# Gated linear attention with a low-rank mixer on one Trainium2 core: another order of the same 2207 operations

## Chip, cores and metric
The kernel runs on one core of a Trainium2 chip. The metric is the device time of one execution in microseconds (us). Before the change the median of three runs is 535.81 us, from 535.58 to 535.88. Five engines take part: PE (TensorE, matrix products), DVE (VectorE), ACT (ScalarE), POOL (GpSimd) and SP (SyncE); the last two mostly issue transfers. Each works off its own row of instructions in order and waits by semaphores for the others.

## What is computed
The first part is a complex gated recurrence per batch (4), head (8) and step (768), with a head dimension of 48, all in float32:

```python
mag = np.sqrt(a_re * a_re + a_im * a_im)
scale = np.minimum(mag, 0.999) / (mag + 1e-06)
...
new_re = ar * S_re - ai * S_im
new_im = ar * S_im + ai * S_re
kv = np.einsum('bhd,bhe->bhde', k[:, :, t], v[:, :, t])
S_re, S_im = (new_re + kv, new_im)
y[:, :, t] = np.einsum('bhd,bhde->bhe', q[:, :, t], S_re)
```

Its result, rearranged to x of 4 x 768 x 384, goes through a token mixer of rank 32 and a channel network:

```python
h = xt @ U @ V
u = x + h.transpose(0, 2, 1)
ch = np.maximum(u @ w_ch1, 0.0) @ w_ch2
return (u + ch).astype(np.float32)
```

Here xt is x with steps and channels exchanged; w_ch1 has 384 x 1536 numbers, w_ch2 1536 x 384.

## The kernel before
The 4 x 768 tokens are cut into 24 chunks of 128 tokens, six to a batch. Twelve groups of two chunks go through the gates together; the mixer and the channel network also take two chunks at a time, so there are twelve of each, called mixer 0 to 11. The stages of a chunk are:

- **Gates** of a group: magnitude and angle of a_re and a_im, on ACT (L459) and DVE; prefix sums over time as products on PE (L751, and L747 where the summand is first split on DVE by L737 and L738; L811, L814, L817 for the angles). L715 to L726 belong to the magnitudes, L820 makes the angles' fraction F. Totals of a chunk go out to memory and back (L762, L765), and L767 keeps their least value.
- **Preparation**: DVE multiplies q and k by the gates' waves (L462), PE transposes (L872), ACT copies to SBUF (L878).
- **Chain**: inner products within a chunk (L901), masked on DVE (L904), products with the state and its update (L921, L951, L959; L462 and L468 on DVE).
- **Mixer**: rank products (L1036, L1109), transposes (L1055), then the channel network: up products (L1074, and L1181, which makes the same sums with fewer products from sums of operands, from mixer 2 on), down products (L1270, L1313, L1484), the additions of their results to xo on DVE (L465), and the transfer of xo to the result: L1257 on POOL, and for the last mixers L1471 on POOL or SP.
- **Weights**: w_ch1 and w_ch2 come as float64 words and are turned into float32 piece by piece on DVE by L611, L615, L617 and a custom instruction of L465 (L459 on ACT for a part). In the rows, w_85 and w_86 are the two matrices.
- **Judging**: small DVE operations, three 1x1 products on PE (L1613 to L1615) and a conversion on DVE (L1617) count the elements whose range the fast way does not cover. Every engine then loads that flag (L1648) and branches (L1658) past a slow version of the whole computation, which is not run with these inputs.
- **Warm-up**: two operations of 7 and 5 products of the identity with itself (L1627), which nothing reads.

The program first collects all of these as 2207 numbered operations, each with its engine, what it reads and writes, and a function that issues its instructions. Nothing is issued until the end, where a method of the plan walks a tuple of numbers called ORDER, which stands at the head of the file:

```python
for n in ORDER if ORDER else range(len(self.ops)):
    assert not self.ops[n][5] - done, "an operation comes before what it needs"
    ...
    done.add(n)
    out += [-1 - n] * SPARE.get(n, 0) + [n]
```

(L159 to L170.) So ORDER alone sets the row of instructions of every engine, and with it in which of its rotating buffers (PSUM banks "bank", the ring "xo", "T", "GS") an operation's result lands. SPARE puts idle products (L1636, L1640) ahead of four named operations; it is not changed. A number in ORDER can only stand behind the operations that it needs.

Of the kernel before, what the change touches and what calls it, by code (L numbers as in the profile page):

```python
# [31 lines left out]
    91, 93, 95, 99, 96, 97, 101, 92, 112, 94, 113, 114, 98, 102, 103, 115, 116, 117, 0, 104, 105, 118, 119, 120, 3, 109, 110, 106, 121, 111, 107, 122,  # L32
    123, 124, 130, 5, 4, 6, 9, 148, 11, 188, 8, 12, 15, 108, 14, 189, 149, 7, 131, 132, 135, 133, 147, 126, 212, 134, 140, 136, 137, 10, 191, 13, 146,
    141, 142, 138, 139, 143, 144, 151, 145, 150, 152, 153, 213, 2, 125, 190, 192, 214, 128, 193, 196, 202, 203, 197, 215, 216, 220, 154, 155, 195,
    204, 194, 156, 127, 199, 198, 17, 2205, 227, 205, 157, 206, 28, 158, 100, 2206, 221, 226, 228, 217, 18, 258, 229, 159, 160, 200, 161, 222, 19, 21,
    223, 219, 16, 164, 218, 162, 163, 166, 20, 165, 29, 309, 172, 173, 1, 201, 207, 224, 22, 225, 283, 259, 23, 208, 30, 31, 32, 33, 261, 308, 231,
    232, 233, 284, 168, 211, 210, 235, 236, 174, 175, 234, 209, 237, 176, 177, 239, 182, 183, 178, 179, 180, 238, 313, 184, 181, 185, 186, 187, 312,
    314, 262, 315, 311, 34, 37, 167, 36, 247, 246, 244, 263, 310, 260, 40, 170, 286, 266, 230, 287, 35, 265, 264, 267, 243, 316, 268, 288, 273, 272,
    317, 290, 269, 270, 318, 248, 46, 351, 319, 240, 241, 289, 42, 271, 350, 291, 292, 285, 26, 25, 320, 321, 322, 47, 245, 293, 294, 274, 323, 324,
    325, 43, 275, 326, 50, 328, 278, 277, 279, 295, 327, 334, 335, 41, 297, 298, 44, 38, 45, 39, 280, 242, 169, 336, 352, 337, 48, 282, 281, 52, 276,  # L40
    299, 49, 296, 338, 300, 340, 54, 339, 344, 329, 330, 586, 51, 345, 302, 303, 353, 341, 304, 375, 253, 252, 342, 343, 588, 376, 398, 346, 354, 305,
    307, 358, 348, 347, 587, 306, 349, 364, 378, 365, 301, 366, 591, 589, 254, 359, 367, 590, 355, 379, 360, 592, 331, 24, 357, 593, 361, 399, 249,
    250, 380, 377, 332, 356, 383, 381, 594, 595, 678, 628, 382, 362, 384, 630, 363, 389, 596, 386, 385, 370, 369, 371, 390, 597, 598, 599, 53, 368,
    391, 387, 388, 702, 600, 601, 602, 27, 629, 633, 55, 392, 393, 394, 372, 374, 58, 373, 397, 396, 677, 395, 400, 401, 402, 603, 403, 606, 404, 604,
    608, 607, 605, 614, 726, 701, 64, 615, 441, 616, 251, 61, 442, 443, 444, 445, 255, 420, 56, 421, 256, 422, 423, 446, 60, 448, 59, 405, 424, 406,
    617, 618, 447, 619, 620, 453, 494, 407, 57, 62, 704, 632, 257, 621, 63, 408, 495, 67, 496, 680, 634, 497, 414, 409, 70, 631, 454, 622, 635, 636,
    66, 65, 68, 610, 71, 76, 459, 460, 623, 73, 129, 624, 451, 637, 638, 415, 72, 498, 410, 639, 452, 640, 609, 82, 625, 641, 77, 69, 74, 75, 642,
    449, 450, 433, 417, 78, 626, 411, 425, 643, 644, 416, 645, 83, 627, 84, 80, 85, 86, 647, 646, 648, 649, 650, 656, 657, 658, 672, 675, 674, 671,
    673, 727, 426, 79, 418, 731, 419, 412, 427, 434, 435, 428, 436, 87, 81, 676, 730, 732, 413, 429, 437, 88, 89, 90, 462, 659, 660, 661, 679, 612,
    662, 438, 430, 729, 663, 733, 681, 685, 664, 439, 705, 651, 703, 825, 728, 611, 776, 502, 734, 691, 692, 682, 499, 503, 693, 463, 694, 665, 666,  # L50
    431, 667, 684, 769, 735, 736, 500, 683, 457, 455, 456, 709, 171, 461, 828, 826, 777, 710, 775, 458, 711, 501, 716, 715, 712, 695, 737, 469, 686,
    717, 800, 504, 778, 827, 505, 738, 706, 652, 653, 668, 739, 669, 707, 801, 688, 687, 708, 740, 470, 466, 471, 467, 506, 741, 718, 742, 803, 472,
    743, 507, 508, 745, 746, 744, 748, 747, 754, 755, 474, 670, 772, 770, 756, 333, 689, 468, 473, 690, 464, 465, 478, 713, 696, 721, 714, 719, 475,
    432, 480, 482, 654, 476, 483, 479, 771, 779, 697, 750, 440, 757, 700, 699, 698, 780, 720, 722, 783, 774, 784, 802, 875, 874, 484, 509, 477, 773,
    485, 510, 511, 758, 486, 515, 724, 759, 785, 723, 829, 782, 760, 490, 781, 804, 481, 725, 761, 516, 808, 805, 786, 512, 762, 513, 830, 514, 809,
    491, 492, 807, 806, 789, 790, 487, 787, 517, 518, 524, 763, 489, 519, 520, 899, 749, 1160, 831, 832, 833, 613, 764, 765, 493, 1161, 526, 528, 525,
    488, 530, 521, 834, 788, 527, 810, 811, 522, 791, 531, 523, 766, 835, 836, 792, 873, 837, 767, 529, 838, 898, 532, 533, 867, 536, 537, 768, 870,
    795, 794, 796, 812, 538, 540, 542, 815, 814, 799, 901, 839, 539, 543, 544, 548, 840, 876, 841, 541, 797, 798, 842, 845, 844, 846, 843, 847, 853,
    869, 854, 868, 546, 545, 813, 549, 793, 552, 816, 817, 553, 550, 547, 534, 535, 1165, 561, 820, 819, 821, 877, 855, 856, 551, 878, 872, 881, 562,
    871, 882, 1162, 848, 849, 752, 822, 824, 857, 858, 823, 879, 902, 880, 906, 558, 887, 888, 900, 850, 883, 859, 860, 554, 884, 1164, 1166, 818,  # L60
    912, 913, 861, 889, 903, 904, 907, 909, 1167, 1209, 1163, 751, 1234, 556, 908, 890, 891, 655, 914, 557, 559, 1168, 563, 862, 753, 863, 885, 886,
    1169, 1203, 905, 910, 911, 560, 893, 892, 564, 555, 566, 1170, 1171, 1172, 1173, 915, 916, 864, 894, 1210, 917, 1259, 1233, 1212, 895, 920, 1236,
    565, 567, 1174, 1175, 1176, 574, 897, 568, 575, 918, 865, 570, 576, 571, 919, 896, 866, 921, 922, 573, 572, 1177, 1179, 1180, 923, 569, 924, 1181,
    1178, 1182, 1188, 1205, 582, 577, 925, 926, 927, 928, 929, 930, 932, 933, 583, 584, 1184, 1261, 1204, 1189, 1207, 1190, 934, 937, 578, 935, 579,
    1211, 1002, 942, 1003, 580, 943, 1191, 940, 936, 1213, 948, 941, 946, 944, 1217, 931, 1214, 1260, 1308, 1206, 1004, 1005, 947, 939, 1006, 1208,
    1262, 1223, 1224, 851, 1307, 1237, 956, 949, 945, 952, 953, 1192, 1225, 1226, 1227, 957, 1215, 1193, 938, 954, 950, 955, 1241, 958, 960, 1194,
    959, 964, 961, 962, 966, 1195, 1258, 1263, 1264, 1216, 1196, 581, 965, 1197, 968, 951, 963, 1235, 969, 967, 1332, 1333, 1248, 1247, 1242, 1265,
    1244, 1007, 970, 1309, 1249, 1243, 1009, 1301, 1335, 1198, 974, 977, 975, 1250, 1199, 1008, 1011, 1200, 978, 972, 971, 1218, 1238, 979, 1219,
    1201, 976, 1012, 1266, 1016, 983, 1267, 973, 986, 1220, 980, 1268, 984, 1269, 982, 981, 1202, 990, 985, 1310, 987, 989, 1270, 1239, 1240, 993,
    1081, 1221, 1245, 988, 1010, 991, 1183, 1358, 994, 1082, 1271, 1015, 1272, 1273, 1274, 1275, 1277, 992, 998, 995, 1083, 1276, 1017, 1019, 1020,  # L70
    1018, 1084, 1014, 1246, 1278, 1279, 999, 1023, 1222, 1251, 1280, 1286, 1302, 1303, 1085, 1000, 1013, 1025, 1026, 1021, 1022, 1311, 1024, 1029,
    1031, 1035, 1027, 1315, 1028, 1032, 1312, 1086, 1287, 1288, 1304, 1305, 1036, 1033, 1034, 1037, 1038, 1281, 1186, 1087, 1088, 1030, 1306, 1314,
    1289, 997, 1001, 1290, 852, 1291, 1041, 1282, 1357, 1405, 1313, 1039, 1043, 1406, 1185, 1292, 1040, 1042, 1293, 1044, 1361, 1294, 1045, 1336,
    1047, 585, 996, 1362, 1048, 1340, 1046, 1316, 1228, 1252, 1253, 1318, 1229, 1254, 1317, 1256, 1230, 1360, 1430, 1319, 1359, 1322, 1334, 1257,
    1321, 1053, 1049, 1408, 1295, 1051, 1323, 1324, 1320, 1232, 1231, 1363, 1255, 1056, 1341, 1337, 1407, 1431, 1296, 1297, 1052, 1050, 1096, 1298,
    1057, 1364, 1365, 1339, 1342, 1054, 1338, 1058, 1343, 1090, 1055, 1366, 1367, 1368, 1062, 1059, 1063, 1060, 1066, 1061, 1326, 1327, 1065, 1097,
    1064, 1399, 1369, 1370, 1371, 1372, 1299, 1300, 1373, 1344, 1328, 1068, 1069, 1072, 1374, 1089, 1091, 1092, 1433, 1070, 1073, 1329, 1376, 1331,
# [1630 lines left out]
```

## Time and profile before

| | us |
|---|---|
| median of three runs | 535.81 |
| the profiled execution's span | 533.9 |
| median less that span | 1.92 |
| PE busy (96% of the span) | 514.2 |
| DVE busy (82%) | 438.2 |
| ACT busy (55%) | 295.8 |
| POOL busy (6%) | 30.5 |

The span to three digits behind the point is 533.889 us. Times in all rows count from its start. Busy time is that of the engine's own instructions; issues of transfers on SP, branches and waits count as none. PEld is PE's loading of weights, which runs beside its products. An arrow in brackets names what ended an engine's idle time.

### The profile page before, as it was taken

How to read it: one execution, taken by the hardware profiler on the slowest of the kernel's cores; microseconds unless marked ns; L12 is line 12 of the kernel's file. 1: busy time of each engine (PE TensorE's matmuls, PEld its weight loads, DVE VectorE, ACT ScalarE, POOL GpSimd, SP SyncE). 2: the span in 40 equal slices, each digit the busy share in tenths (PEclk: the TensorE clock that was granted, in tenths of full speed). 3: DMA queues.
4: the chain of work that ended last, by engine and by line, in shares of the span. 5: the costliest groups of instructions: out<-in, count | busy, mean ns of one | idle time of the engine just before them, and what ended most of it. 6: DMA issues, size and time to landing. Idle time of an engine off the chain costs nothing.

```text
span 533.9 us, 17164 instructions
## 1 busy us (share of the span) xinstructions
PE 514.2 (96%) x7494; PEld 468.1 (88%) x7494; DVE 438.2 (82%) x863; ACT 295.8 (55%) x531; POOL 30.5 (6%) x58
## 2 busy tenths in 40 slices
PE   2899999999999999999999999999999999999996
PEld 1777786757989989999999999999999999999996
DVE  7898988999999998897886887786878866877842
ACT  5889998893776866546647655543555412221000
POOL 1000000001020001001100001100010000000010
PEclk9999999999999999999999999999999999999999
DMA  9967985565233423601534150500240000000002
GB/s 226 206 114 194 191 145 163 171 107 112 41 75 92 63 46 80 111 1 29 118 53 83 33 106 25 98 9 23 47 70 26 2 2 1 1 2 1 1 28 97
DMA packets 150706, 39.95 MB, mean 75 GB/s; under 512 B 145880, under 2 KB 147440, under 8 KB 150624
## 3 DMA queue, kind: packets, MB, share of 16 engines
q1 hardware_dynamic: 148544, 34.63, 32.3%
q0 software_dynamic: 2080, 4.15, 2.3%
q8 instruction: 61, 1.00, 0.8%
q14 instruction: 21, 0.17, 0.1%
HBM read 33.60 MB, written 4.76 MB: 72 GB/s over the span
## 4 chain that ended last, share of the span: by engine, by line
PE 81%; DVE 11%; ACT 3%; issue 2%; DMA 2%; SPq 0%; DVEq 0%; ACTq 0%
PE down L1313 20%; PE few L1181 13%; PE bank L1181 12%; PE bank L1484 7%; PE bank L872 4%; PE bank L901 4%; PE up L1074 3%; PE bank L959 3%; PE bank L921 3%; PE bank L951 2%; DVE QKC L462 2%; PE bank L1036 1%; PE bank L747 1%; PE bank L751 1%; PE bank L811 1%
## 5 line engine op out<-in xcount | busy, mean ns | idle before, releaser
L878 ACT COPY QK<-bank 112x512 f32<-112x512 f32 x96 | 51.8, 591 | 18.2 <-PE bank L872 17.9
L1313 PE MATMUL down<-w,h 128*128 128x192 f32 x288 | 53.6, 331 | 0.0
L462 DVE TENSOR_TENSOR QKC<-qk,cs 128x768 f32<-128x768 f32 x48 | 45.0, 951 | 4.9 <-ACT cs L459 4.7
L459 ACT ACTIVATE gate<-gate 128x768 f32<-128x768 f32 (+1 forms) x50 | 39.8, 798 | 16.3 <-DVE wide L719 12.7
L1313 PEld LDWEIGHTS down<-w,h 128*128 128x128 f32 x288 | 47.0, 190 | 0.9
L465 DVE TENSOR_TENSOR xo<-bank,xo 128x192 f32<-128x192 f32 x78 | 25.3, 350 | 24.9 <-PE bank L1484 16.0
L1189 ACT COPY h<-few 128x512 f32<-128x512 f32 x35 | 20.3, 585 | 30.0 <-PE few L1181 29.9
L1074 PE MATMUL up<-uT,w 128*128 128x256 f32 x144 | 34.0, 385 | 0.2
L456 ACT ACT_TABLE_LOAD x24 | 30.8, 1283 | 1.1 <-PEq L1692 0.7
L1074 PEld LDWEIGHTS up<-uT,w 128*128 128x128 f32 x144 | 26.6, 190 | 5.0 <-DVE xo L465 0.5
L1181 PE MATMUL bank<-extra,w 128*128 128x128 f32 x232 | 30.3, 276 | 0.0
L872 PE MATMUL bank<-ident,QKC 64*112 64x64 f32 x768 | 29.1, 221 | 1.0 <-DVE G L468 0.4
L872 PEld LDWEIGHTS bank<-ident,QKC 64*112 64x112 f32 x768 | 24.4, 130 | 6.2 <-DVE QKC L462 1.4
L459 ACT ACTIVATE es<-bank 128x384 f32<-128x384 f32 x48 | 20.3, 495 | 16.6 <-PE bank L747 15.8
L797 POOL DMA_DIRECT2D gate<-F x15 | 12.5, 832 | 285.2 <-DVE F L820 167.2
L1181 PEld LDWEIGHTS bank<-extra,w 128*128 128x128 f32 x232 | 28.3, 192 | 0.1
L1313 PE MATMUL down<-stage 128*128 128x192 f32 x144 | 28.0, 332 | 0.2 <-DVE xo L465 0.2
L465 DVE TENSOR_TENSOR xo<-down,xo 128x192 f32<-128x192 f32 (+1 forms) x58 | 22.0, 386 | 7.1 <-PE down L1313 6.9
L901 PE MATMUL bank<-QK 112*64 112x64 f32 x768 | 26.6, 224 | 0.0
L901 PEld LDWEIGHTS bank<-QK 112*64 112x64 f32 x768 | 24.2, 138 | 1.3 <-issue 0.5
L459 ACT ACTIVATE cs<-F 128x384 f32<-128x384 f32 x48 | 23.3, 516 | 3.0 <-DVE F L820 2.9
L1313 PEld LDWEIGHTS down<-stage 128*128 128x128 f32 x144 | 23.5, 190 | 1.2 <-DVE xo L465 0.5
(249 smaller groups left out, 1228.6 us busy)
## 6 DMA issues: line engine op xcount, KB each, us to landing
stage<-in_moe_w_ch_dram SPq DMA_DIRECT2D x12, 768.0 KB
gate<-in_a_re_dram SPq DMA_DIRECT2D x24, 192.0 KB
gate<-in_a_im_dram SPq DMA_DIRECT2D x24, 192.0 KB
qk<-in_q_dram SPq DMA_DIRECT2D x24, 192.0 KB
qk<-in_k_dram SPq DMA_DIRECT2D x24, 192.0 KB
VP<-in_v_dram SPq DMA_DIRECT2D x24, 192.0 KB
out_dram<-xo POOLq DMA_DIRECT2D x13, 192.0 KB, 2.9
out_dram<-xo POOLq DMA_DIRECT2D x16, 96.0 KB, 2.5
```

The costliest lines, as they stand in the source:

```text
L456: ACT(1.4, rank, lambda: nc.scalar.preload_act_table_set(name), writes=[TABLE])
L459: return nc.scalar.activation(out=o, in_=i, func=f, **kw)
L462: nc.vector.tensor_tensor(out=o, in0=a, in1=b, op=OP.mult)
L465: nc.vector.tensor_tensor(out=o, in0=a, in1=b, op=OP.add)
L872: nc.tensor.transpose(out=get(*ps[r])[0:DQ, h], in_=get(*qkc)[at, h].rearrange("p u d -> p (u d)")[:, 0:DQ], identity=ident[at, at], tile_ ...
L878: nc.scalar.copy(out=get(*QK)[0:DQ, u].rearrange("p (h t) -> p h t", t=CH)[:, :, r * HC:(r + 1) * HC], in_=get(*ps[r])[0:DQ])
L901: nc.tensor.matmul(out=get(*ps0)[r:r + HC, h], lhsT=k_of(h, r, HC), rhs=q_of(h, r, HC), start=True, stop=True, tile_position=(0, r))
L1074: nc.tensor.matmul(out=get(*ps)[:, e], lhsT=w1[:, f, (ff + e) * 128:(ff + e + 1) * 128], rhs=get(*uT)[:, f], start=(f == 0), stop=(f == KD ...
L1181: nc.tensor.matmul(out=get(*ps)[:, q], lhsT=w()[:, q * 128:(q + 1) * 128], rhs=v[0](), start=(n == 0 and q == 0), stop=True, skip_group_ch ...
L1189: ACT(c_act(n3 * CH) - 0.045, RU, lambda i=i, k=k: nc.scalar.copy(out=at(i, k), in_=get(*ps)), [ps], [o])
L1313: nc.tensor.matmul(out=get(*to)[:, part], lhsT=x(j), rhs=y[:, j], start=(first and j == 0), stop=(j == KH - 1), skip_group_check=not first)
L1484: nc.tensor.matmul(out=get(*ps), lhsT=w[0]()[:, q], rhs=x[0]()[:, q], start=(n == 0 and q == 0), stop=(q == k3 - 1), skip_group_check=True)
```

## The change
Only the tuple ORDER is another one: the same 2207 numbers, 2144 of them in another place. It was found by replaying the program three times with the durations of the other engines than PE varied. The file has one line fewer, so every line number of the changed kernel is lower by one than the same line before.

```diff
 ORDER = (
-    91, 93, 95, 99, 96, 97, 101, 92, 112, 94, 113, 114, 98, 102, 103, 115, 116, 117, 0, 104, 105, 118, 119, 120, 3, 109, 110, 106, 121, 111, 107, 122,
...
-    2182, 2179, 2183, 2161, 2180, 2184, 2188, 2189, 2185, 2186, 2191, 2174, 2099, 2094, 1687, 2102, 2190, 2192, 2187, 2193, 1686, 1691, 2194, 2195,
-    2196,
...
+    2188, 2184, 2189, 2191, 2194, 2195, 2192, 2185, 2186, 2080, 2081, 1686, 1687, 2102, 2094, 1691, 2190, 2193, 2187, 2196, 2203, 2204, 2099,
 )
```

The rows of the engines show what it moves. PE's first products before (prefix sums of the first two chunks, idle products, angles):

```order
L751 MATMUL bank_61<-GL,prefix_r 128x384
L1636 MATMUL bank_62<-ident 128x128 x2
L751 MATMUL bank_62<-GL,prefix_r 128x384
L1636 MATMUL bank_63<-ident 128x128 x10
L814 MATMUL bank_63<-gate,prefix_z 128x384
```

And PE's first products now:

```order
L1626 MATMUL warm<-ident 128x128 x12
L750 MATMUL bank_61<-GL,prefix_r 128x384
L1635 MATMUL bank_62<-ident 128x128 x2
L750 MATMUL bank_62<-GL,prefix_r 128x384
L1635 MATMUL bank_63<-ident 128x128 x10
```

Both warm-up operations, which stood behind the first chunk's state products, now stand ahead of everything on PE.

On DVE, the place where the first group with a split summand (group 6) is split, before; GL is the summand, GS its two parts:

```order
L904 COPY_PREDICATED AT_130<-mask,bank_65 128x512
L723 SCALAR_TENSOR_TENSOR GL<-gate,GL 128x768
L462 TENSOR_TENSOR G<-G,T_121 112x384
L468 ISA GM<-bank_62,G 112x384
L904 COPY_PREDICATED AT_132<-mask,bank_65 128x512
L726 SCALAR_TENSOR_TENSOR GL<-GL,gate 128x768
L737 CAST GS_107<-GL 128x768
L738 TENSOR_TENSOR GS_108<-GL,GS_107 128x768
```

And the same place now:

```order
L464 ISA w_86<-w_86,stage 128x1536
L722 SCALAR_TENSOR_TENSOR GL<-gate,GL 128x768
L461 TENSOR_TENSOR G<-G,T_121 112x384
L614 TENSOR_SCALAR stage<-stage 128x768
L467 ISA GM<-bank_61,G 112x384
L903 COPY_PREDICATED AT_130<-mask,bank_62 128x512
L903 COPY_PREDICATED AT_132<-mask,bank_63 128x512
L725 SCALAR_TENSOR_TENSOR GL<-GL,gate 128x768
L736 CAST GS_107<-GL 128x768
L737 TENSOR_TENSOR GS_108<-GL,GS_107 128x768
```

Pieces of the second weight matrix (w_86 and its stage) are now unpacked ahead of the split; before, they stood behind it.

The end of POOL's row before, with the last transfers of xo and the load of the flag:

```order
L1471 DMA out_dram<-xo_128 128x384
L1471 DMA out_dram<-xo_127 128x384
L1257 DMA out_dram<-xo_126 128x192
L1471 DMA out_dram<-xo_127 128x384
L1257 DMA out_dram<-xo_126 128x384
L1257 DMA out_dram<-xo_126 128x192
L1648 TENSOR_LOAD flag
```

And now:

```order
L1256 DMA out_dram<-xo_126 128x384
L1256 DMA out_dram<-xo_126 128x192
L1470 DMA out_dram<-xo_127 128x384 x2
L1256 DMA out_dram<-xo_126 128x192
L1470 DMA out_dram<-xo_128 128x384
L1647 TENSOR_LOAD flag
```

The transfer of xo_128, which is chunk 20, stood ahead of five others and is now the last. It waits for DVE's additions to xo_128, whose row at the end now reads:

```order
L464 TENSOR_TENSOR xo_128<-bank_61,xo_128 128x192
L464 TENSOR_TENSOR xo_128<-bank_62,xo_128 128x192
L1616 CAST flag<-bank_63 1x1
L1647 TENSOR_LOAD flag
```

The end of PE's row before:

```order
L1484 MATMUL bank_66<-w_86,hq 128x192 x4
L1484 MATMUL bank_63<-w2x,w_85 128x192 x4
L1484 MATMUL bank_64<-w2x,w_85 128x192 x4
L1484 MATMUL bank_66<-gate,hq 128x192 x4
L1648 TENSOR_LOAD flag
```

And now:

```order
L1483 MATMUL bank_61<-w2x,w_85 128x192 x4
L1483 MATMUL bank_62<-w2x,hq 128x192 x4
L1612 MATMUL bank_63<-ones,bad 1x1
L1613 MATMUL bank_63<-ones,wide 1x1
L1614 MATMUL bank_63<-ones,bad 1x1
L1647 TENSOR_LOAD flag
```

The last full products belong to chunk 20 (operation 2080; 2081 is its addition and 2099 its transfer), and the three products of the flag (2203; 2204 is the conversion), which stood eight operations of L1484 ahead of the end, now follow them.

165 rows, old and new, of the table ORDER are left out of this document.

## Prediction, made blind
> **What bounds the kernel now.** The page comes first: the span and the busy shares.
>
> ```profile
> span 533.9 us, 17164 instructions
> PE 514.2 (96%) x7494; PEld 468.1 (88%) x7494; DVE 438.2 (82%) x863; ACT 295.8 (55%) x531; POOL 30.5 (6%) x58
> ```
>
> PE (TensorE) is busy for 514.2 of 533.9 us. The other 19.7 us, and what makes PE's own work longer or shorter, are all that a new order can touch. Where the 19.7 us lie is in the view of busy time by stretch (columns: stretch, length, busy time of PE, PE's weight loads, DVE, ACT, POOL, then granted clock, DMA share and GB/s):
>
> ```profile
> 0.00:16.65 16.65, 5.70 (x29) 4.50 (x29) 12.70 (x35) 10.90 (x20) 1.94 (x14) 1.00 0.94 215
> 16.65:82.40 65.75, 63.88 (x1308) 51.08 (x1308) 58.83 (x95) 58.86 (x106) 0.00 (x0) 1.00 0.82 176
> 200.00:447.00 247.00, 246.62 (x3867) 235.77 (x3866) 200.15 (x414) 127.27 (x238) 17.53 (x27) 1.00 0.26 50
> 447.00:528.94 81.94, 81.94 (x640) 80.46 (x638) 54.41 (x116) 10.73 (x19) 3.21 (x6) 1.00 0.05 17
> 528.94:533.89 4.95, 0.00 (x1) 0.00 (x0) 0.36 (x1) 0.00 (x0) 0.00 (x0) 0.81 0.22 70
> ```
>
> PE stands for 11 us at the start, nearly 2 in the stretch up to 82.40, 0.4 in the 247 us from 200, not at all in the last 82 before 528.94, and again for the **4.95 us behind its last product**. So the middle and the late part can only be shortened by making PE's work shorter. The start, the first 80 us (where DVE and ACT are at 90% beside PE) and the end are the places for waits.
>
> **Term 1: the start.** The timeline of the start (start, length, engine, line, operation, count; in brackets the idle time ahead and what ended it):
>
> ```profile
> 1.23 0.57 SPq L569 DMA_DIRECT2D gate<-in_a_im_dram  x1
> 2.72 0.85 SPq L569 DMA_DIRECT2D gate<-in_a_im_dram  x1
> ```
> ```profile
> 10.18 1.62 PE L751 MATMUL bank<-GL,prefix_r 128*128 128x384 f32 x2 [10.18 <-DVE GL L465]
> 11.59 1.06 PE L1636 MATMUL bank<-ident 128*128 128x128 f32 x4
> 12.44 1.20 PE L751 MATMUL bank<-GL,prefix_r 128*128 128x384 f32 x2
> 13.48 2.39 PE L1636 MATMUL bank<-ident 128*128 128x128 f32 x20
> 16.65 1.56 PE L814 MATMUL bank<-gate,prefix_z 128*128 128x384 f32 x4 [0.77 <-ACT gate L459]
> 25.18 1.83 PE L1627 MATMUL warm<-ident 128*128 128x128 f32 x14
> 27.48 1.38 PE L1627 MATMUL warm<-ident 128*128 128x128 f32 x10
> ```
>
> The two warm-up operations of L1627 take 1.83 + 1.38 = 3.2 us of PE at 25 to 29 us. The change puts them ahead of the first L751, where PE stands until 10.18 anyway, so **3.2 us of PE's work go**, hidden under the first loads. The first loads also change places: the pair of a_re and a_im that was issued second (done being issued at 3.57, against 1.80) now comes first. I put the work that follows on the first products 0.3 us later, a fifth of the 1.5 us between the two issues. The bounds: half of those 1.5, +0.75; and -0.74 if the early warm-up leaves PE's first products at the later speed. That is what the rows give: the first two L751 take 1.41 us from start to the next start and the second two 1.04; the first four idle products take 0.85, and twenty of the same 2.39, which for four is 0.48. So 0.37 + 0.37 are there to win. PE waits for ACT at 16.65, so little of it should arrive, and I take none.
>
> The Trainium skill, "TensorE: Matmul & The Clock Gate", section "What's actually happening", states that the array runs at half its clock by default and again after an idle window of about 3.4 us, and at the full clock after about 3.4 us of work. The trace agrees in that the same idle product falls from 0.21 to 0.12 us within 4 us of the first work. By that rule the warm-up lies too early if it ends more than about 3.4 us ahead of the first product and the first products stay slow, so the sum stays as it is; if it ends later, the sum would be the one with -0.74.
>
> **Term 2: the early stretch is bounded by DVE.** After the start, the first 65 us run from DVE's first F to the end of the L738 that splits group 6:
>
> ```profile
> 18.21 0.55 DVE L820 SCALAR_TENSOR_TENSOR F<-F,bank 128x384 f32<-128x384 f32 x1 [1.83 <-ACT F L459]
> 18.68 0.95 DVE L465 CUSTOM_DVE_ANT_0 w<-w,stage 128x1536 uint16<-128x1536 uint16 x1
> ...
> 82.39 0.96 DVE L738 TENSOR_TENSOR GS<-GL,GS 128x768 fp32r<-128x768 f32 x1
> ```
> ```profile
> 18.21:83.36 65.15, 62.76 (x1305) 50.60 (x1305) 59.78 (x95) 58.23 (x104) 0.00 (x0) 1.00 0.81 174
> ```
> ```profile
> L615 DVE TENSOR_SCALAR stage<-stage 128x768 uint16<-128x768 uint16 (+1 forms) x13 | 7.5, 587 | 0.0
> L617 DVE TENSOR_SCALAR w<-w 128x768 uint32<-128x768 uint32 x12 | 6.6, 556 | 0.5 <-ACT w L459 0.3
> L767 DVE TENSOR_TENSOR least<-least,T 112x16 f32<-112x16 f32 x12 | 2.0, 167 | 0.0
> ```
>
> In before the stretch lasts 65.15 us, with PE busy 62.76, DVE 59.78 and ACT 58.23. The new order has five more instructions on DVE ahead of that L738: one L767 (0.17), and four that unpack the second weight matrix: two L615 (0.59 each), one L617 (0.56), one custom L465 (0.95). That is 2.9 us by their durations; an instruction overlaps the next one by some 0.1 us (18.21 to 18.68 for a length of 0.55), so 2.4. DVE then has 62.2 us. PE has 3.2 less (the warm-up), 1.8 less by term 3, and one more up product (1.4, below): 62.76 - 3.6 = 59.2. DVE becomes the busiest. In before the stretch was 2.4 us longer than its busiest engine; with the same 2.4 it lasts 64.6, and ends at 18.5 + 64.6 = 83.1 against 83.36, **0.3 earlier**. So nearly everything that PE gains here is eaten by DVE. The bounds: DVE without any idle time (62.2 us, ends at 80.7, 2.7 earlier) and DVE with all the 5.4 us that it stands idle now (65.15 - 59.78; ends at 86.1, 2.75 later).
>
> One up product more is done by then, taken from behind the place. The chain of waits shows six of its matmuls:
>
> ```profile
> 87.45 1.49 PE up L1074 x6
> ```
>
> They take about 1.4 to the next start, so PE has **1.4 us less** to do after the place.
>
> **Term 3: PE changes its kind of product less often.** Where PE goes from one shape to another, the distance from start to start is longer than within a kind:
>
> ```profile
> 168.22 1.16 PE L1181 MATMUL few<-extra 128*128 128x128 f32 x8
> 169.22 1.06 PE L1181 MATMUL bank<-gate,w 128*128 128x128 f32 x8
> 170.11 1.06 PE L1181 MATMUL few<-extra,gate 128*128 128x128 f32 x8
> 171.10 0.94 PE L921 MATMUL bank<-VP,QKC 64*48 64x48 f32 x64
> ```
>
> Eight L1181 take 0.89 us between their own kind (169.22 to 170.11), 1.00 when entered from another kind (168.22), 0.99 when left for L921 (171.10): about 0.11 a switch. I counted the switches in PE's two orders, with transposes, inner products, state products, rank products and full 128x128 products as kinds: 249 in before, 214 in the new order; 16 of the 35 fewer lie up to the place of term 2, 19 behind it. Those 19 save 19 x 0.11 = **2.1 us**, since PE is never idle there; the 16 (1.8 us) are in term 2's PE work. Bounds: nothing, and 35 x 0.11 = 3.9.
>
> Sum of the terms for PE's last product: -0.3 - 1.4 - 2.1 = **-3.8 us**, so it ends at 525.1. Bounds from term 2: -6.2 without waits, -0.75 with all of them.
>
> **Term 4: the end.** What follows the last product, on each engine:
>
> ```profile
> 518.03 0.62 DVE L465 TENSOR_TENSOR xo<-bank,xo 128x192 f32<-128x192 f32 x2 [2.24 <-PE bank L1484]
> ...
> 528.98 0.36 DVE L465 TENSOR_TENSOR xo<-bank,xo 128x192 f32<-128x192 f32 x1 [0.94 <-PE bank L1484]
> ```
> ```profile
> 518.95 0.54 POOL L1471 DMA_DIRECT2D out_dram<-xo  x1 [9.35 <-DVE xo L465]
> ...
> 520.54 1.07 POOL L1257 DMA_DIRECT2D out_dram<-xo  x2
> ```
> ```profile
> L1658 POOLq EVENT_SEMAPHORE  x5: 17/43/2272, 521.4 to 524.0; - x5
> L1658 POOLq INC_SWDGE_SEM  x1: 1063/1063/1063, 524.0 to 524.0; - x1
> L1658 PEldq COMPARE_BRANCH  x2: 90/1878/3665, 526.5 to 529.1; - x2
> ```
> ```profile
> L1703 POOLq DRAIN  x3: 46/112/3728, 527.9 to 533.6; - x3
> L1703 PEldq DRAIN  x2: 8/38/68, 532.9 to 533.4; - x2
> ```
>
> (The last two fences give, for a line, count: shortest/median/longest ns, first and last start.) In before PE sets the end: its branch behind the last product takes 3.67 us, its drain comes at 532.9, and a common close of about 1.0 us follows. POOL starts its last two transfers at 520.54, so the second at 521.07, eight us ahead of the last product, and its own closing work lies beside PE's: a wait of 2.27 for the landing, 1.06 of counter update up to 525.1, nothing until 527.9, a drain of 3.73 up to 531.6. From the start of its last transfer to the end of that drain POOL needs 531.64 - 521.07 = **10.6 us**.
>
> The new order takes this cover away. The products of chunk 20 (the operation numbered 2080) become PE's last full ones, DVE's additions to that chunk's xo come behind them, and POOL's last transfer, which writes that chunk out, waits for them. So POOL's closing work starts only there: the addition starts 0.04 us after the product and takes 0.36, POOL starts its transfer 0.30 after that (518.65 to 518.95), then 10.6, then the close of 1.0: 12.3 us after the last product, where now it is 4.95. **Term 4 is +7.3 us.** The three 1x1 products that count the flag, and its conversion, also move to the end; flag, load and branch on PE then take 5 to 6.5 us after the last product and are no longer last.
>
> The bounds: if the long drain is in truth a wait for the other engines' transfers (it ends about where SyncE's last transfer lands), 3.73 go and the term is +3.6. If the gap of 2.8 ahead of it goes too, only landing and counter remain (4.0 in place of 10.6): +0.8. I take the full length, since no other engine has so long a drain and POOL's gap and drain follow its own branch.
>
> The Trainium skill, "Runtime: NRT & Kernel Launch", section "Instruction fetch mechanics", says that a taken branch to code outside the loaded pages waits until that page is fetched. The trace agrees: 2.8 us lie between POOL's branch and its drain. By that rule the gap belongs to POOL and comes after its branch wherever that stands, so the +0.8 would be out of reach.
>
> **Sum.** 533.89 - 3.8 + 7.3 = 537.4 for the span. The median of the runs, 535.81, is 1.92 above the profiled span; with the same 1.92 the forecast is **539.3 us**, 0.65% slower. A measurement of this kernel can tell about 0.2% (1.07 us) from no change.
>
> **Rivals.** *The end stays covered (faster).* One mechanism, at POOL's queue: its drain and the gap ahead are waits that end with the other engines, so only landing and counter count, +0.8: 533.89 - 3.8 + 0.8 + 1.92 = 532.8. For it speaks that the drain ends as SyncE's last landing is due; against it the branch ahead of the gap. It decides as soon as the close takes under 4.95 + 3.8 = 8.75 us after the last product. Chance 0.15; with DVE without idle time besides (-6.2), 530.4, chance 0.08. *Only the drain is a wait*: +3.6, 535.6, no difference; chance 0.12. *DVE waits as much as now, with more work*: -0.75 + 7.3, 542.3; for it speaks that ACT and PE feed DVE as they do now, against it that PE has less to do there; chance 0.13. *DVE never waits*: -6.2 + 7.3, 536.9; chance 0.10. My forecast has 0.42.
>
> **How the numbers follow.** The range goes from 532.3 to 542.8: it leaves out the 530.4 and the far side of the 542.3. Slower by over 0.2% (above 536.9): 0.42, 0.13, and half of the 0.10: 0.60. Within: the other half and most of the 0.12: 0.14. Faster: 0.15, 0.08 and the rest: 0.26.
>
> **What would show it.** Step by step: the two L1627 rows ahead of the first L751, which still starts between 9.5 and 11; the L738 of group 6 ending within 80.7 to 86.1, with DVE busy about 62 us from its first F; PE's last full product between 522.7 and 528.2; POOL's last issue behind DVE's last addition, and behind it a landing wait, a gap and a drain of 3.7 us with the span's end 12 us after the last product. The prediction is wrong if the drain shrinks to some tens of ns, if DVE's added unpacking falls into its idle time, or if new waits of PE show up between 200 and 520.

## The result and the profile after

The changed kernel takes 540.67 us (median of four runs, 539.75 to 541.79), the kernel before 535.80 (535.58 to 535.88): a ratio of 1.0094, 95% interval 1.0078 to 1.0109. It is slower by 0.9%; forecast were 539.3 us within 532.3 to 542.8. The profiled execution took 541.31 us, and its runs lie further apart than those of before (2.0 us against 0.3).

The head of the page after:

```profile
span 539.4 us, 17174 instructions
PE 513.6 (95%) x7494; PEld 470.9 (87%) x7494; DVE 437.5 (81%) x863; ACT 295.2 (55%) x531; POOL 30.5 (6%) x58
```

PE is busy for 0.6 us less, and the span is 5.5 us longer. Busy time by stretch, with the columns as in the prediction:

```profile
0.00:16.65 16.65, 10.58 (x46) 9.21 (x47) 12.03 (x35) 10.12 (x18) 1.94 (x14) 0.79 0.90 205
16.65:83.00 66.35, 61.97 (x1291) 49.30 (x1289) 63.04 (x102) 62.09 (x111) 0.00 (x0) 1.00 0.87 190
200.00:447.00 247.00, 246.84 (x3846) 237.33 (x3845) 198.88 (x413) 127.65 (x240) 17.12 (x26) 1.00 0.25 47
447.00:525.00 78.00, 78.00 (x607) 77.35 (x607) 55.65 (x120) 9.59 (x17) 2.68 (x5) 1.00 0.04 13
```
```profile
525.94:539.40 13.46, 0.23 (x7) 0.12 (x6) 0.41 (x2) 0.00 (x0) 0.54 (x1) 0.70 0.13 41
```

The last row is the loss: 13.46 us follow the last full product, where before 4.95 did. That is +8.5, against -3.0 for the product itself (528.94 to 525.94); together they are the 5.5. Two things are new besides: the granted clock of the start is 0.79, where the row of before says 1.00 (its first products were slow too, four idle ones in 0.85 us against twenty in 2.39 behind them), and DVE is the busiest engine of the early stretch.

What stands behind the last product, from the timeline and from the rows of the sequencers (count: shortest/median/longest ns, first and last start):

```profile
524.48 1.46 PE L1483 MATMUL bank<-w2x,hq 128*128 128x192 f32 x8
...
525.99 0.36 DVE L464 TENSOR_TENSOR xo<-bank,xo 128x192 f32<-128x192 f32 x1 [0.94 <-PE bank L1483]
526.26 0.13 DVE L1616 CAST flag<-bank 1x1 int32<-1x1 f32 x1
526.89 0.54 POOL L1470 DMA_DIRECT2D out_dram<-xo  x1 [9.84 <-DVE flag L1616]
```
```profile
L1657 POOLq EVENT_SEMAPHORE  x5: 17/43/3169, 527.5 to 531.0; - x5
...
L1657 POOLq COMPARE_BRANCH  x2: 38/39/40, 527.4 to 532.2; - x2
...
L1657 POOLq INC_SWDGE_SEM  x1: 1063/1063/1063, 531.1 to 531.1; - x1
```
```profile
L1702 POOLq DRAIN  x3: 46/112/3728, 534.8 to 539.1; - x3
...
L1702 PEldq DRAIN  x2: 8/38/68, 531.0 to 538.9; - x2
```

POOL's row reads like a list of what the last transfer pays for: issue at 526.89, landing wait of 3.17, counter update of 1.06, branch at 532.2, nothing until 534.8, drain of 3.73 until 538.5. PE is ready at 531.0 and waits 7.5 us for POOL in the common close.

### The profile page after: what moved, and what is told of

It reads as the page before. It is cut to its first block, busy times and chain, and to the rows that moved or that the text cites. A ratio compares the mean times of both kernels' runs of the same rounds, so it can differ in the third digit from the quotient of the medians.

```text
span 539.4 us, 17174 instructions
## 1 busy us (share of the span) xinstructions
PE 513.6 (95%) x7494; PEld 470.9 (87%) x7494; DVE 437.5 (81%) x863; ACT 295.2 (55%) x531; POOL 30.5 (6%) x58
## 3 DMA queue, kind: packets, MB, share of 16 engines
q0 software_dynamic: 2080, 4.15, 2.3%
## 5 line engine op out<-in xcount | busy, mean ns | idle before, releaser
L1312 PE MATMUL down<-w,h 128*128 128x192 f32 x288 | 52.2, 331 | 0.0
L871 PE MATMUL bank<-ident,QKC 64*112 64x64 f32 x768 | 27.7, 220 | 2.2 <-DVE QKC L461 1.8
L1256 POOL DMA_DIRECT2D out_dram<-xo x26 | 17.2, 732 | 129.7 <-DVE xo L464 95.9
```

Source lines behind the costliest of these rows:

```text
L871: nc.tensor.transpose(out=get(*ps[r])[0:DQ, h], in_=get(*qkc)[at, h].rearrange("p u d -> p (u d)")[:, 0:DQ], identity=ident[at, at], tile_ ...
L1256: queue.dma_start(out=out[b, c * CH:(c + 1) * CH, lo:hi], in_=get("xo", i)[:, lo:hi])
L1312: nc.tensor.matmul(out=get(*to)[:, part], lhsT=x(j), rhs=y[:, j], start=(first and j == 0), stop=(j == KH - 1), skip_group_check=not first)
```

## Experiments

All were run beside the kernel before on the same chip. In experiments 1, 2, 3 and 5 all line numbers are 7 higher than in the kernel before; in the others they are those of the kernel before. The diffs of ORDER show only the numbers that move and some beside them.

**1. The tail as before.** The last 138 operations go back to the relative order that they had before.

```diff
 ORDER = (
...
-    2185, 2186, 2080, 2081, 1686, 1687, 2102, 2094, 1691, 2190, 2193, 2187, 2196, 2203, 2204, 2099,
+    2185, 2186, 2191, 2174, 2099, 2094, 1687, 2102, 2190, 2192, 2187, 2193, 1686, 1691, 2194, 2195, 2196,
 )
```

> The changed order up to its 2069th operation, and the last 138 operations in the order that they had before (chunk 20's down products, its transfer and the flag's products early again). Theory (POOL's closing work, laid bare, is what the change loses): the last product stays some 3 us earlier than in the kernel before and about 5 us follow it, so the time is 532 to 534 us, below the kernel before (535.8). Rival 1 (the loss lies in PE's 1.8 us of standing and the slow products at 85 to 91 us, and the tail costs little): 538 to 540. Rival 2 (the close is long for another reason than the place of the last transfer): no change, 540.7.

Measured: 532.66 us (531.63 to 535.47), ratio 0.9952 (0.9934 to 0.9970). Its rows at the end:

```profile
524.79 1.46 PE L1491 MATMUL bank<-gate,hq 128*128 128x192 f32 x8
```
```profile
L1710 POOLq DRAIN  x3: 46/112/3729, 524.9 to 530.9; - x3
L1710 SPq DRAIN  x3: 7/7/7, 530.2 to 530.6; - x3
...
L1710 PEldq DRAIN  x2: 8/38/68, 530.1 to 530.6; - x2
```

POOL's drain of 3.73 us now starts at 524.9, beside PE's last products, and is over before PE (530.1) and SyncE (530.2) are ready: 4.9 us follow the last product (526.25 to a span of 531.1). Some 8 us come back, so the tail is the whole of the loss, and without it the changed order is 0.5% *faster* than before.

That SyncE is ready 0.1 us behind PE holds for the kernel before as well, where the prediction names PE alone (532.9):

```profile
L1703 SPq DRAIN  x3: 7/7/7, 533.0 to 533.3; - x3
```

**2. The last transfer on SyncE.** The changed order as it is; only the issuing queue of chunk 20 differs.

```diff
-                if t:
+                if t or n == 20:
                     SP(0.6, ("load", 0), lambda: f(nc.sync), [o], [("out", n)])
```

> The changed order as it is, but chunk 20's transfer, still the last, is issued by SyncE in place of POOL. Theory (POOL's own closing work counts from its last transfer on): POOL's last transfer is then issued at about 516.5 us and its close is over before PE's; what follows the last product is PE's flag, branch and the common close, 6 to 8 us in place of 13.5, so 533.5 to 535.5 us. Rival (POOL's long drain is a wait for the last landing of any queue): the drain still ends some 5 us behind the last transfer, 537 to 540.

Measured: 538.52 us (534.26 to 540.12), ratio 1.0035 (1.0011 to 1.0060). The trace is of a run at 538.4. The theory expected 533.5 to 535.5 and missed; the rival's number came, but not for the rival's reason:

```profile
L1665 POOLq EVENT_SEMAPHORE  x5: 17/42/43, 527.7 to 528.0; - x5
...
L1665 POOLq COMPARE_BRANCH  x2: 38/39/40, 527.6 to 529.2; - x2
...
L1665 POOLq INC_SWDGE_SEM  x1: 1043/1043/1043, 528.1 to 528.1; - x1
```
```profile
L1710 SPq EVENT_SEMAPHORE  x14: 17/28/28, 529.1 to 536.6; - x14
...
L1710 SPq DRAIN  x3: 7/7/7, 529.9 to 536.1; - x3
L1710 POOLq DRAIN  x3: 46/112/3647, 532.1 to 536.4; - x3
...
L1710 DVEq DRAIN  x2: 10/34/58, 531.1 to 536.1; - x2
L1710 PEldq DRAIN  x2: 8/38/67, 531.8 to 536.1; - x2
```

The landing wait is gone (43 ns), yet POOL's first branch stands at 527.6: it cannot come before the flag, and the flag's conversion runs at 526.86 in this trace. From the flag on POOL goes through counter, branch, gap and drain as before. And the drain of 3.65 starts at 532.1, when SyncE has passed its own wait for the last landing (its semaphores run on from 529.1, its drain at 529.9) and DVE and PE stand at their drains (531.1 and 531.8): nothing is left to land, and the view of transfers has nothing but instruction packets from 528.5 on. **The drain is POOL's own time**, not a wait for a transfer or another engine, which answers what the prediction had left open between its bounds.

**3. The tail of the change in the order before.**

```diff
-    2080,
...
-    2081,
...
-    2203,
...
-    2204,
...
-    2099,
...
     2194, 2195, 2196,
+    2080, 2081, 2203, 2204, 2099,
```

> The order before with five operations moved to its end, as the change has them: chunk 20's last products, their addition, the flag's products, its conversion, and last POOL's transfer of chunk 20. Theory: the end moves by the bare close of POOL, 8 to 9 us, so 543.5 to 545 us. Rival (only the landing and the counter count, as the prediction's short bound had it): 536 to 537. Rival (the drain is a wait): 539 to 540.5.

Measured: 544.82 us (544.24 to 545.17), ratio 1.0168 (1.0151 to 1.0185), so +8.9 on the kernel before beside it (535.91) with nothing else of the change; the prediction's term has +7.3. It is the theory's number; both short bounds of the prediction are out.

**4. The flag alone at the end**, because of experiment 2:

```diff
-    2203,
...
-    2204,
...
     2194, 2195, 2196,
+    2203, 2204,
```

> The order before with only the flag's three products and its conversion moved to the very end; chunk 20 and its transfer stay early. Theory (POOL's close begins when POOL may branch, and its branch waits for the flag, as the run with the last transfer on SyncE suggests): POOL's counter update, gap and drain of some 8.5 us start at the flag, about 0.8 us behind the last product, so the time is 539.5 to 541.5 us. Rival (as the prediction had it, only the last transfer on POOL starts the close): 535.8 to 537, since PE's own flag, branch and close take 5 to 6 us.

Measured: 541.74 us (541.69 to 542.05), ratio 1.0113 (1.0097 to 1.0130): +5.9, a little above the theory's range. Its POOL row: branch at 530.0, counter at 530.5, branch at 531.6, drain at 535.7:

```profile
L1703 POOLq DRAIN  x3: 46/112/3728, 535.7 to 540.0; - x3
```

So the late flag would have cost 5.9 us by itself; the late transfer adds 3 us (544.82 less 541.74). By the two traces that is a landing wait of 3.28 and a first branch 0.9 later, less a gap ahead of the drain that is 1.2 shorter (4.0 here, 2.8 in experiment 3). The prediction had named only the transfer, and had called the flag "no longer last" because it followed it on PE alone.

**5. The warm-up alone moved to the front**, in the order before (operation 109 is PE's first product):

```diff
+    2206, 2205,
     109,
...
-    2205,
...
-    2206,
```

> The order before, with the two warm-up operations alone moved ahead of PE's first product, as the change has them. Theory (DVE and ACT bound the first 80 us, and PE's clock falls again while it waits for its first data): of the 3.2 us taken from PE little arrives, the first products run up to 1 us slower: 535 to 536.5 us. Rival (PE's work sets the time there too): 532.5 to 533.5 us.

Measured: 537.48 us (536.60 to 538.04), ratio 1.0032 (1.0018 to 1.0047): 1 us above the theory's upper end, slower than before. The place that the two operations left:

```profile
27.45 0.57 PE L928 MATMUL bank<-VP,QKC 64*48 64x48 f32 x32 [1.74 <-ACT QK L885]
29.33 0.26 PE L879 MATMUL bank<-ident,QKC 64*112 64x64 f32 x1 [1.30 <-DVE GM L939]
...
31.88 2.06 PE L1647 MATMUL bank<-ident 128*128 128x128 f32 x10
```
```profile
30.00:33.50 3.50, 3.47 (x55) 3.25 (x56) 3.17 (x7) 3.24 (x6) 0.00 (x0) 0.52 0.72 141
```

Of the 3.2 us taken away, 1.74 + 1.30 = 3.04 come back at the same place as waits for ACT and DVE. And after these waits the granted clock is 0.52 for 3.5 us: ten idle products take 2.06 us where they took 1.38 before. The two operations had filled a wait and kept the clock up; at the front they do neither.

**6. The warm-up back among the waits** (the tail as before too; 197 is the second chunk's transposes, 200 the inner products behind them):

```diff
-    2206, 2205,
...
+    2206,
     197,
...
+    2205,
     200,
```

> The changed order with the last 138 operations as before, and the two warm-up operations put back among PE's waits at 24 to 28 us. Theory (in their old place they cost nothing, since PE waits there anyhow, and they keep its clock up): no stretch of clock 0.50 after 20 us, the spread of the runs shrinks, 530 to 531.8 us. Rival (the prediction's first term: 3.2 us of PE's work come back): 534.5 to 536.

Measured: 532.80 us (531.70 to 535.83), ratio 0.9954 (0.9937 to 0.9971): the same as experiment 1. Neither time came: 3.2 us of PE's work do not come back (rival out), no clock of 0.50 is left in its trace up to the last product (as expected), and the time and the spread stay. The spread has another cause, and the loss that experiment 5 shows in the order before is not seen in the changed order, where the two operations cost the same at either place.

**7. A longer warm-up**, so that PE does not stand ahead of its first product:

```diff
-    WARM = (7, 5)
+    WARM = (28, 5)
```

> The changed order with the last 138 operations as before, and the first of the two warm-up operations four times as long (28 products in place of 7), so that PE has work from 1.4 to about 10.8 us and does not stand ahead of its first product. Theory (PE's clock falls in the 4 us in which it stands there): no clock of 0.50 between 9 and 16 us, the angles' first product 0.6 to 1 us earlier, 531.5 to 532.3 us. Rival (the first products are slow whatever stands ahead of them, or wait for data in any case): 532.7, unchanged.

Measured: 533.20 us (531.28 to 537.96), ratio 0.9956 (0.9923 to 0.9990): inconclusive on the time. On the mechanism it is clear: no clock of 0.50 in its trace up to the last product, the first two products of L751 in 0.81 us instead of 1.62 (experiment 1), and the angles' first product at 16.52 instead of 17.23. In exchange PE stands for "issue" in four places, 3.1 us in all.

**8. The late part alone.** The first 410 operations and the last 138 in the order before, the changed order between.

> The first 410 operations and the last 138 in the order before, those between in the changed order: what the changed order brings between 84 and 515 us. Theory (fewer changes of kind, 19 of them, at 0.11 us): 2 to 3 us below the kernel before, 532.8 to 534 us. Rival (the gain of the changed order lies in the first 84 us): 535.5 to 536.

Measured: 540.30 us (539.90 to 540.82), ratio 1.0090 (1.0073 to 1.0107). It tells nothing about the late part: at the seam a product of L1091 waits 5.7 us for DVE (L1085), and the clock falls to 0.50 from 92 to 99 us. Two orders cannot be spliced there.

**9 and 10. The wait for instructions.** In the changed kernel PE stands for 1.84 us at 85.5, and the view names no cause:

```profile
84.80 0.70 PE L1035 MATMUL bank<-r,V 32*128 32x96 f32 x16
87.35 2.59 PE L1073 MATMUL up<-uT,w 128*128 128x256 f32 x6 [1.84 <-issue]
89.86 1.19 PE L1035 MATMUL bank<-r,V 32*128 32x96 f32 x16
```
```profile
87.00:91.00 4.00, 3.65 (x25) 2.50 (x25) 0.68 (x1) 1.61 (x3) 0.00 (x0) 0.57 1.05 268
```

Weights for the up product are loaded at 85.43, the product itself starts at 87.35, and then the clock is 0.57: the six up products take 2.59 us where six took 1.56 before, the sixteen spread products 1.19 instead of 0.70. With the standing that is some 3.4 us. The view of transfers has a queue for instructions, and the quarter of a microsecond from 85.00 holds one packet of it, the first since 78.25:

```profile
q8 instruction: 1, 0.02, 22.9%
```

Between these two packets PE ran 430 instructions (2292 to 2722, weight loads included), while 250 was usual at other places. The suspicion: the packet was due earlier and lay behind the eleventh piece of the weights, which SyncE had issued at 80.19. (In the kernel before the packet is as late, at 82.75 after 430 instructions since 76.50, and PE does not stand: it had waited for DVE at 83.4 and reaches the packet's instructions later.) The first kernel cuts that transfer to a quarter:

```diff
-                out=get("raw", p)[:, at:end].rearrange("p (c m) two -> p c (m two)", c=a.shape[1]), in_=a.bitcast(U32)),
+                out=get("raw", p)[0:(32 if p == 10 else 128), at:end].rearrange("p (c m) two -> p c (m two)", c=a.shape[1]), in_=a.bitcast(U32)[0:(32 if p == 10 else 128)]),
```

> The changed order with the last 138 operations as before; of the eleventh piece of the weights, whose load starts at about 80 us, only 32 of 128 rows are loaded (the other rows keep what stood there, so that part of w_ch2's values is left out). Theory (PE stands at 85.5 us because the load of its next instructions, due at about 81.5, waits behind this transfer and starts only at 85.0): the packet of instructions starts before 83.5, PE's standing of 1.6 to 1.8 us ahead of the up product at 87.5 is gone, and the median falls by 1.5 to 3 us to 529.7 to 531.2, with a smaller spread. Rival (the standing belongs to that place of the program, whatever the transfers do): it stays, 532.7.

Measured: 532.29 us (531.57 to 532.82), ratio 0.9933 (0.9916 to 0.9949). The packet starts at 84.5, later than expected, and the standing is halved to 0.82 us; the clock stays at 1.00 behind it. The second kernel puts the transfer and the one after it later in SyncE's row:

```diff
-    70,
...
-    76,
...
     610,
+    70, 76,
```

> The changed order with the last 138 operations as before, and the loads of the eleventh and twelfth piece of the weights placed behind one more issue of SyncE that waits until 85.5 us; nothing is left out. Theory: as with the quarter of the load, the packet of PE's instructions starts before 83.5 and the standing at 85.5 to 87.5 goes: 530 to 531.5 us. Rival 1 (the standing stays or comes back at the next packet of instructions, which then meets the moved load): 532.7. Rival 2 (the unpacking of the eleventh piece now waits, and DVE with it): 533 to 535.

Measured: 532.28 us (531.12 to 532.79), ratio 0.9940 (0.9924 to 0.9957). Here the packet starts at 82.50, and there is no standing:

```profile
85.00 0.70 PE L1036 MATMUL bank<-r,V 32*128 32x96 f32 x16
85.63 1.56 PE L1074 MATMUL up<-uT,w 128*128 128x256 f32 x6
```

The six up products start 0.63 us behind the sixteen before them and take 1.56 again. That fits the suspicion, but does not show it: it is one trace of each kernel, and others speak against it. Experiment 2, with the whole transfer in its place, stands at the same product for the 0.82 us of the quartered load:

```profile
89.50 1.45 PE L1081 MATMUL up<-uT,w 128*128 128x256 f32 x6 [0.82 <-issue]
```

And of the two kernels with a longer warm-up, in which the standing falls on another product, experiment 7 has the loads in their place and experiment 11 (below) has them later; their standings hardly differ, though next to nothing is transferred in the second:

```profile
83.53 0.53 PE L995 MATMUL rank<-xo,UV 128*32 128x96 f32 x13 [1.11 <-issue]
```
```profile
83.34 0.36 PE L995 MATMUL rank<-xo,UV 128*32 128x96 f32 x5 [0.93 <-issue]
```
```profile
82.00:84.00 2.00, 1.02 (x13) 0.58 (x10) 1.95 (x5) 1.61 (x4) 0.00 (x0) 1.00 0.03 3
```

What holds wherever PE stands so is the link to the packet: PE goes on 2.2 to 3.0 us after it began. What makes the packet late stays open. The median of experiments 9 and 10 is only 0.4 us below that of experiment 1, less than expected, and the intervals overlap. The traces differ in the clock of the start as well (0.50 until 16 us in these two, until 14 in experiment 1, which has another such stretch from 27.6 to 31). The runs lie within 1.3 and 1.7 us, where experiment 1 has 3.8, but they are four runs each against ten.

**11 and 12. All of it together**: the tail as before, the loads later, and the warm-up once longer (24 and 5 products at the front), once among the waits.

> The changed order with the last 138 operations as before, the loads of the eleventh and twelfth piece of the weights later, and the first warm-up operation of 24 products in place of 7, so that PE has work until about 11 us. Theory (three losses of the changed order are separate and each is now taken away: the bare close of POOL, the wait for instructions at 85 us, the slow clock at 9 to 16 us): the angles' first product at about 16.5 us, no clock of 0.50 in the trace, 530.3 to 531.5 us with a spread of under 2 us. Rival (what the start wins is lost again in DVE's and ACT's first 80 us): 532.0 to 532.5, as with the later loads alone.

> The same, but the two warm-up operations as they were (7 and 5 products), put among PE's waits at 24 to 28 us. Theory (at that place they cost some 0.4 us and the first products run slow): 531 to 532.3 us, 0.3 to 1 us above the kernel with the long warm-up. Rival (the place of the warm-up matters only through the clock after 27 us): equal to it or below.

Measured: 534.25 us (533.19 to 536.26), ratio 0.9977 (0.9960 to 0.9994), for the first; 532.82 us (531.18 to 533.36), ratio 0.9935 (0.9919 to 0.9951), for the second. The long warm-up does what it should at the start (angles' first product at 15.85), and loses it later: PE stands for "issue" five times, 3.4 us in all, and the clock is 0.50 again at 85 to 88 us. That its 34 more matmul rows and as many weight loads are instructions to be fetched too would fit, but was not tried by itself. The theory that the losses are separate thus fails. The best kernels that compute everything are experiment 10 and the last one, 0.6% below the kernel before; their intervals overlap that of experiment 1.

## Why the prediction was right, and where its sizes were off

**The end (term 4): right in place and sign, 1.2 us too small.** Forecast +7.3, measured +8.5 (13.46 less 4.95). From the last transfer's issue to the drain's end POOL took 11.6 us (526.89 to 538.53) against the 10.6 taken over from before; the landing wait alone was 3.17 in place of 2.27, and POOL's issue came 0.95 behind the last product in place of 0.70. The bounds below (+3.6 and +0.8), and with them the rival of the other sign, fall with experiments 2 and 3: drain, gap and counter are POOL's own. What the term missed is that the flag's place alone lays most of this bare (experiment 4).

**The start (term 1): the step failed in size.** It gave 0.3 us, with 0.75 as its bound. Measured:

```profile
1.40 4.93 PE L1626 MATMUL warm<-ident 128*128 128x128 f32 x24 [1.40 <-POOL ident masks.py:199]
11.00 1.62 PE L750 MATMUL bank<-GL,prefix_r 128*128 128x384 f32 x2 [4.67 <-DVE GL L464]
...
14.54 3.02 PE L1635 MATMUL bank<-ident 128*128 128x128 f32 x20
17.55 1.56 PE L813 MATMUL bank<-gate,prefix_z 128*128 128x384 f32 x4
```
```profile
9.00:15.00 6.00, 4.00 (x11) 2.82 (x12) 3.97 (x9) 4.29 (x10) 0.00 (x0) 0.50 0.99 254
```

The warm-up ends at 6.33, PE stands for 4.67 us, and the granted clock is 0.50 from 9 to 15 us. The angles' first product starts 0.9 us later than before (17.55 against 16.65), and 0.82 of it is there already at the first product (11.00 against 10.18), which waits for DVE's data. That comes with the new order of loads and gates and not with the warm-up: 10.22 in experiment 5, 11.13 in experiment 6. It is the size that the term had wrong, by more than its bound allowed. The slow clock adds next to nothing: from the first product to the angles' it takes 6.55 us against 6.47, since the wait of 0.77 for ACT is gone. The rule cited ahead from the Trainium skill, "TensorE: Matmul & The Clock Gate", section "What's actually happening", agrees with these rows in the half clock, and its consequence, no gain at the first products, came; the clock was down at 9.0 already, 2.7 us after the warm-up's end. That 3.2 us of PE's work go is right for PE's busy time (term 2), and the sum rightly gave it no time: experiment 5 shows that 3.04 of them had filled waits.

**The early stretch (term 2): right at its end, with two errors that cancel.** DVE's first F and the split of group 6:

```profile
19.11 0.55 DVE L819 SCALAR_TENSOR_TENSOR F<-F,bank 128x384 f32<-128x384 f32 x1 [1.06 <-ACT F L458]
...
81.87 0.96 DVE L737 TENSOR_TENSOR GS<-GL,GS 128x768 fp32r<-128x768 f32 x1
```
```profile
19.10:82.83 63.73, 59.35 (x1279) 47.91 (x1278) 61.47 (x100) 60.10 (x106) 0.00 (x0) 1.00 0.86 189
```

The stretch lasts 63.7 us with DVE busy 61.5, 2.3 above its busiest engine; forecast were 64.6, 62.2 and 2.4. PE has 59.35, forecast 59.2. The split ends at 82.83, forecast 83.1; that it lies so near is partly luck, for the stretch began 0.6 us later than forecast (19.11 against 18.5) and was 0.9 shorter. That DVE bounds it fits its busy time; no run changes DVE's work alone.

**Behind that place (term 3 and the up product): right in sign, too small, and hidden by a loss that was not foreseen.** From the split to the last product:

```profile
83.36:528.94 445.58, 444.17 (x6157) 412.37 (x6157) 365.33 (x732) 225.76 (x406) 28.57 (x44) 1.00 0.27 55
```
```profile
82.83:525.94 443.11, 440.96 (x6169) 412.23 (x6158) 362.23 (x726) 223.16 (x405) 28.00 (x43) 1.00 0.27 53
```

The first row is before, the second now: -2.5, where -3.5 was forecast. The forecast said that PE is never idle there; before it was idle for 1.4 us, and now for 2.15, of which 1.84 are the standing at 85.5. PE's own work is 3.2 us shorter, though the slow products behind the standing cost 1.5; without them it would be 4.7, so 1.2 us more than forecast. The forecast's share for changes of kind stands: counted on the products of the two traces, 18 fewer lie behind the place (153 before, 135 now), where it had 19, though its totals of 249 and 214 are lower there (200 and 171). The standing and the slow products, which the forecast put at nothing, hide some 3.4 us.

Where the 1.2 come from is not shown. It is not a change between down products of 192 columns and others of 128, which the count took for one kind: six down products ahead of such a change take 0.98 us to the next start, 0.163 each, and 0.163 is also the distance within their own kind.

```profile
285.69 1.14 PE L1313 MATMUL down<-w,more 128*128 128x192 f32 x6
286.67 1.05 PE L1181 MATMUL bank<-extra,w 128*128 128x128 f32 x8
```

**The sum.** -3.8 + 7.3 = +3.5 was forecast; -3.0 + 8.5 = +5.5 was measured in the profiled execution, and +4.9 in the medians. Two errors of 0.8 and 1.2 us, both towards a shorter time, make up the difference; in the 0.8, errors of both signs have partly cancelled.

## What to carry to other kernels

When an order is changed, look at what closes the program on each queue, not only at the engine that is busy: here a transfer and a flag, both tiny, were put last, and an idle engine's close cost 8.5 us where the order had won 3. Before filler work is moved out of a busy engine, look at what it stands in: if PE waits there, nothing is won, and its clock can fall (experiment 5; in the changed order the place made no difference). An unexplained "issue" wait of PE is worth a look at the queue of instructions.

## What the runs showed that was not expected

- POOL's drain at the end takes 3.65 to 3.74 us in every trace, whether or not anything is left to land; its counter update 1.04 to 1.06, and 2.5 to 4.0 us pass between its last branch and the drain.
- In the traces of the kernel before and of experiments 3, 4 and 5 PE stands 0.2 to 0.4 us for "issue"; in those that begin with the changed order mostly 1.5 to 3.4. Every standing for "issue" that the timelines of the fourteen traces list ends 2.2 to 3.0 us after a packet began on its instruction queue, also where hardly anything else is transferred (0.70 us ahead of 417.96 in experiment 7, with a DMA share of 0.01 from 414 to 418). The runs of these kernels also lie 1.3 to 6.7 us apart, those of experiments 3 to 5 within 1.5. The Trainium skill, "Runtime: NRT & Kernel Launch", section "Instruction fetch mechanics", calls the cost of fetching the next block mostly hidden; these traces agree for most packets (some 60 in each), and not for those ahead of these standings.
- In these traces PE's granted clock stays the same for 3.4 us or a multiple of it. It fell to 0.50 behind stretches of that length in which PE had been busy for less than half: 0.73 of 3.4 us ahead of 9.0 in the changed kernel, and 1.56 of 3.4 ahead of 87.5 (the row below), where it stood for only 1.84. In experiment 1 it fell behind 24.2 to 27.6 with 48% and stayed behind 85.7 to 89.1 with as much. Behind stretches with more it stayed, but for one: in experiment 11 it fell at 85.3 with PE busy for 71%.

```profile
84.10:87.50 3.40, 1.56 (x27) 1.17 (x20) 2.54 (x7) 3.38 (x7) 0.00 (x0) 1.00 0.60 196
```
